# Fetching the first half's turned tiles earlier, and another order of the last batch's four sums

## The chip, the cores and the metric

One Trainium2 chip, one of its cores. The time is device microseconds (us) of one execution of the whole program, inputs and outputs in HBM. The kernel before takes 1034.33 us (median of 3 runs, 1034.21 to 1034.42). The engines are TensorE (PE; its weight loads are PEld), VectorE (DVE), ScalarE (ACT), GpSimd (POOL) and SyncE (SP), which here issues nearly all transfers, in the order of its queue.

## The reference

Sparse attention over 4 batches of 8 heads, 768 positions and 64 channels, followed by a Fourier mixing block. Cut to what is computed:

```python
scores = (q @ k.T) / sqrt(64)                 # per head, 768 x 768
scores = where(mask, scores, -1e9)            # window, first and last blocks, random blocks
attn = softmax(scores) ; x = attn @ v         # heads side by side: x is (4, 768, 512)
mixed = real(fft(fft(x, axis=1), axis=2))
u  = x + mixed
un = (u - mean(u)) / sqrt(var(u) + 1e-6)      # over the 512 channels
out = u + max(un @ w_ch1, 0) @ w_ch2          # w_ch1 is 512 x 2048, w_ch2 2048 x 512
```

## The kernel before

The program runs one batch after another, numbered 0 to 3 here. A batch's attention goes by pairs of heads. While TensorE does the attention of the next batch, the engines carry out the mixing and the two dense layers of the batch before; the last batch's mixing stands alone at the end. A batch's 768 rows are held as two halves, 0 and 1, of three tiles of 128 rows by 512 channels (T is 3).

The order of the work is made when the program is built. A planner keeps three lists. `apart` holds the mixing steps of a batch in a fixed order (`before`, then `after`); `late` holds the dense layers of the batch, eight products `quad` with rounds of `channels` in between (`outputs` in the last batch); `short` holds small steps of the attention. It places their steps between the attention's matmuls by rough costs. Each engine then runs its instructions in exactly the order in which they were written, and waits at the head of its queue.

What the change touches lies between the mixing and the first dense product. The normalised rows `un` must be turned, so that channels lie along the partitions (tile `unT`, one for each half):

- In batches 0 to 2 `un_blocks` (L1021) turns 32 x 32 blocks on VectorE (L1026) and stores the tile to a scratch area in HBM (`far<-un`, L1027). `fetch` (L1031) brings a half back in four pieces of 192 KB (`unT<-far`, L1040). A fetch must wait until the three stores of its half have landed. The six tiles come in the order half 0: 1, 2, 0, then half 1: 1, 2, 0.
- When the first tile of half 1 is stored and at most five items of the batch before are left in `late`, `fetch(0, True)` does not issue the pieces of half 0 but puts them in the list `parts`. They are issued two at a time behind a store of results of a half 0 (`store`, L1306), and whatever is left goes out in `un_back` (L1050), which stands behind the last tile of half 1 and fetches half 1 as well.
- In batch 3 `un_flip` turns the tiles with TensorE and ScalarE copies them (L1009); nothing goes through HBM.

Then `right` (L1071, its instruction is L1085) forms four sums over the turned tiles of both halves, called R1 to R4 here: R1 and R2 give t1 and t2 (the tile `t`), R3 overwrites a part of half 1's `unT`, R4 gives t4 and needs R2's t2. In batches 0 to 2 each of them is one instruction over all three tiles; in batch 3 each is two, a wide one for tiles 1 and 2 and a narrow one for tile 0.

`quad` (L1110) is a product of 2 x 2 blocks in seven matmul groups of four (L1131). Its groups come in this order: `xp` and `yp` from half 0's `unT` alone, `z` from t2, `z` from t1, `z` from R3's result (into the PSUM bank of the first z, and so behind VectorE's addition of it, `hA`, L1136), `yp` from t4, and a last `z`.

Of the kernel before, what the change touches and what calls it, by code (L numbers as in the profile page):

```python
# [104 lines left out]
def kernel(  # L105
# [29 lines left out]
    T = C // 2  # L135
# [858 lines left out]
    def mixer(b, xA, xB):  # L994
# [3 lines left out]
        first, pq, ar, sp, wh = fourier(b, xA, xB, uns)  # L998
        tt = nc.vector.tensor_tensor

        def un_flip(half, m):
            if half not in unT:
                unT[half] = tr_p.tile([P, ND, T * P], FP32, tag="tr", name="unT")
            un = uns.pop((half, m))
            tag, pool = (("t", ps_t), ("m", ps_m))[half == 1 and m != 0]
            tp = pool.tile([P, ND, P], FP32, tag=tag, name="utp")
            for d in range(ND):
                nc.tensor.transpose(tp[:, d, :], un[:, d * P:(d + 1) * P], ident)
            nc.scalar.copy(out=unT[half][:, :, m * P:(m + 1) * P], in_=tp)  # L1009
# [11 lines left out]
        def un_blocks(half, m):  # L1021

            un = uns.pop((half, m))
            if half not in lines:
                lines[half] = far_p.tile([T, P, DM], FP32, tag=f"un{half}", name="far")
            nc.vector.transpose(out=un, in_=un)  # L1026
            by["dma"].dma_start(out=lines[half][m], in_=un)  # L1027
            if half == 1 and len(late) < 2 * T:
                fetch(0, True)

        def fetch(half, by_parts=False):  # L1031

            if half in unT:
                return
            unT[half] = tr_p.tile([P, ND, T * P], FP32, tag="tr", name="unT")
            of = lines[half].rearrange("m (g j) (k a i) -> a j k (m g) i",
                                       j=BLK, a=P // BLK, i=BLK)

            def part(a):
                by["dma"].dma_start(  # L1040
                    out=unT[half][BLK * a:BLK * a + BLK].rearrange(
                        "j k (g i) -> j k g i", i=BLK),
                    in_=of[a])
            for a in range(P // BLK):
                if by_parts:
                    parts.append(lambda a=a: part(a))
                else:
                    part(a)
# [22 lines left out]
        def right(j, *tiles):  # L1071

            spare_room()
            if 1 not in t:
                both = room(4, [P, ND, HS], "t12")
                t[1], t[2], t[3] = both[:, K1, :], both[:, K2, :], unT[1][:, K1, :]
            b11, b21 = unT[0][:, K1, :], unT[0][:, K2, :]
            b12, b22 = unT[1][:, K1, :], unT[1][:, K2, :]

            def part(ap):  # L1080
                return ap.rearrange("p k (t n) -> p k t n", n=P)[:, :, tiles[0]:tiles[-1] + 1, :]

            to, a, c = {1: (t[1], b12, b11), 2: (t[2], b22, t[1]), 3: (b12, b22, b12),
                        4: (t[4], b21, t[2])}[j]
            tt(out=part(to), in0=part(a), in1=part(c), op=ALU.subtract)  # L1085
# [292 lines left out]
        def outputs(r, m, after):  # L1378
# [71 lines left out]
            if r == 1:  # L1450
# [3 lines left out]
        fl = [[("tm"[h == 1 and m != 0], lambda h=h, m=m: un_flip(h, m), 0.6, 0.55, 0.0)  # L1454
               for m in range(T)]
              for h in range(2)]

        ft = [[("d", lambda h=h, m=m: un_blocks(h, m), 0.0, 0.0, 0.7) for m in range(T)]
              for h in range(2)]

# [3 lines left out]
        ri = [[("d", lambda i=i, m=m: right(i, *m), 0.0, 0.0, us) for i in (1, 2, 3, 4)]  # L1464
              for m, us in (((1, 2), RIGHT), ((0,), COMBINE))]
        le = [("d", lambda i=i: left(0, i), 0.0, 0.0, COMBINE) for i in (1, 3, 4)]
        after = ([fl[0][1], sp[1][1]] + le +
                 [fl[0][2], sp[1][2], wh[1][1], fl[0][0], sp[1][0], wh[1][2],
                  fl[1][1], fl[1][2], wh[1][0]] + ri[0] + [fl[1][0]] + ri[1])
        if not last:  # L1470
            before = first + [pq[1], ar[0][1], ar[1][1], sp[0][1],
                              pq[2], wh[0][1], ft[0][1], ar[0][2], ar[1][2], sp[0][2],
# [31 lines left out]
    short, apart, late, due = deque(), deque(), deque(), deque()  # L1504
# [82 lines left out]
    def begin(b):  # L1587


        before, after, rest = mixer(b, x_of[b, 0], x_of[b, 1])  # L1590
        any_of = len(late) + len(apart) + 4 * len(rest)
        hold = 2 * T
        apart.extend((*step, any_of) for step in norm_steps(b) + before)
        apart.extend((*step, hold) for step in after)

        def go():
            late.extend(rest)
        apart.append(("-", go, 0.0, 0.0, 0.0, hold))
# [202 lines left out]
    def general():  # L1801
# [5 lines left out]
        for b in range(B):  # L1807
            xs = [xp.tile([P, T, DM], FP32, tag=tag, name="x") for tag in ("xA", "xB")]
            for h in range(H):
# [43 lines left out]
                for half, x in enumerate(xs):  # L1853
                    sl = slice(half * T, half * T + T)
                    nc.vector.tensor_tensor(out=x[:, :, h * D:(h + 1) * D], in0=op[:, sl, :],
                                            in1=rs[:, sl, :].broadcast_to([P, T, D]),
                                            op=ALU.mult)
            before, after, rest = mixer(b, *xs)
            for step in before + after:
                step[1]()  # L1860
# [44 lines left out]
```

## Time and profile before

| | |
|---|---|
| median of 3 runs | 1034.33 us |
| the profiled execution, its own time | 1034.89 us |
| its span, first to last instruction | 1033.2 us |
| mean granted clock of TensorE | 0.997 |
| TensorE busy | 1011.1 us, 98% |
| VectorE, ScalarE, POOL busy | 713.4, 372.9 and 329.5 us |
| pieces fetched (`unT<-far`) | 24, in the six fetches of batches 0 to 2 |
| share of the 16 transfer engines, SP's and ScalarE's queue together | 26.3% |

In the timelines a row gives start and length in us, engine, line, operation, output and inputs, shape and count; in brackets stands how long the engine sat idle before it and who ended that. Rows of neighbouring instructions of one kind are merged. `SPq` is SP's queue: the row shows how long SP was taken up with issuing, not when the data landed. In rows of stretches (A:B) the busy time and the count of PE, PEld, VectorE, ScalarE and POOL follow the length, then the granted clock of TensorE (1.00 is full speed), the transfer engines' busy share and GB/s.

### The profile page before, as it was taken

The numbers are of one execution on the slowest core, as the hardware profiler recorded it, in microseconds if no ns is written. First come the engines' busy times: TensorE is split into PE (matmuls) and PEld (weight loads), VectorE is DVE, ScalarE is ACT, GpSimd is POOL, SyncE is SP. The second block draws the span as 40 slices with busy tenths as digits, with TensorE's granted clock in tenths as the row PEclk, the third lists the DMA queues.
The fourth block names the chain that finished last, engine by engine and source line by source line (L and its number), as shares of the span: only waits on it lengthen the run. The fifth ranks groups of instructions, "written<-read, shape, count | busy, mean of one in ns | idle before, by whom it ended". The sixth has DMA issues, their size and how long they took to land.

```text
span 1033.2 us, 13060 instructions
## 1 busy us (share of the span) xinstructions
PE 1011.1 (98%) x4526; PEld 561.3 (54%) x4526; DVE 713.4 (69%) x1294; ACT 372.9 (36%) x763; POOL 329.5 (32%) x363
## 2 busy tenths in 40 slices
PE   8999999999999999999999999899999999999997
PEld 4434345444767764443534764444444765578576
DVE  6899895977984767755678578565458565675664
ACT  6998765563222222433440223243220221210210
POOL 1000183657634314544552233256540221000000
PEclk9999999999999999999999999999999999999999
DMA  7867422283000008432320002931010001200001
GB/s 216 227 192 229 107 48 46 52 131 49 1 1 1 11 10 166 89 62 40 67 48 1 1 11 85 144 56 43 16 23 8 1 1 51 41 1 0 1 13 53
DMA packets 182309, 60.46 MB, mean 59 GB/s; under 512 B 163018, under 2 KB 173012, under 8 KB 182236
## 3 DMA queue, kind: packets, MB, share of 16 engines
q1 hardware_dynamic: 181116, 58.95, 26.1%
q8 instruction: 38, 0.62, 0.2%
q10 hardware_dynamic: 1088, 0.59, 0.2%
q14 instruction: 35, 0.29, 0.1%
q0 software_dynamic: 32, 0.01, 0.0%
HBM read 46.14 MB, written 15.73 MB: 60 GB/s over the span
## 4 chain that ended last, share of the span: by engine, by line
PE 79%; DVE 10%; ACT 2%; issue 2%; SPq 2%; DMA 2%; POOL 1%; ACTq 0%; DVEq 0%; POOLq 0%
PE z L1131 16%; PE y L1298 13%; PE s L587 10%; PE o L661 9%; PE yp L1131 7%; PE yy L1392 7%; PE xp L1131 4%; PE yz L1239 3%; PE zp L869 2%; PE yc L1239 2%; SPq L1040 2%; PE yw L1239 2%; PE sp L732 1%; DVE x L939 1%; DVE t L1085 1%
## 5 line engine op out<-in xcount | busy, mean ns | idle before, releaser
L647 POOL TENSOR_TENSOR acc<-acc,e 128x384 f32<-128x384 f32 x160 | 164.1, 1059 | 91.8 <-DVE e L617 72.2
L587 PE MATMUL s<-qT,kT 64*128 64x384 f32 x768 | 153.4, 514 | 5.4 <-ACT e L607 3.7
L661 PE MATMUL o<-e,vr 128*64 128x384 f32 x768 | 142.2, 497 | 0.0
L617 DVE TENSOR_TENSOR e<-s,mask 128x768 f32<-128x768 f32 x86 | 78.2, 950 | 47.7 <-ACT s L615 39.7
L587 PEld LDWEIGHTS s<-qT,kT 64*128 64x128 f32 x768 | 63.8, 185 | 85.9 <-ACT e L607 22.6
L647 POOL TENSOR_TENSOR acc<-e 128x384 f32<-128x384 f32 x42 | 47.7, 1157 | 191.4 <-ACT e L607 121.1
L615 ACT ACTIVATE s<-s 128x768 f32<-128x768 f32 x86 | 65.2, 791 | 107.3 <-PE s L587 107.1
L607 ACT ACTIVATE e<-s 128x768 f32<-128x768 f32 x106 | 80.9, 811 | 52.0 <-PE s L597 34.1
L1131 PE MATMUL z<-unT,t 128*128 128x384 f32 x256 | 93.7, 489 | 2.0 <-DVE hA L1136 2.0
L661 PEld LDWEIGHTS o<-e,vr 128*64 128x64 f32 x768 | 47.7, 136 | 69.8 <-issue 68.5
L1136 DVE TENSOR_TENSOR hA<-z,hA 128x384 f32<-128x384 f32 x64 | 35.6, 556 | 63.9 <-PE z L1131 63.9
L1140 ACT ACTIVATE hA<-hA 128x384 f32<-128x384 f32 x64 | 33.5, 523 | 128.2 <-DVE hA L1136 128.2
L1252 POOL TENSOR_TENSOR x<-of,x 128x256 f32<-128x256 f32 x45 | 39.2, 876 | 124.8 <-ACT of L1244 61.7
L1298 PE MATMUL y<-w_sb,hB 128*128 128x512 f32 x168 | 75.4, 597 | 0.0
L1298 PE MATMUL y<-w_sb,hA 128*128 128x512 f32 x168 | 74.6, 596 | 0.0
L1131 PEld LDWEIGHTS z<-unT,t 128*128 128x128 f32 x256 | 48.6, 191 | 37.8 <-DVE hA L1136 4.7
L1140 ACT ACTIVATE hB<-hB 128x384 f32<-128x384 f32 x64 | 33.5, 523 | 87.3 <-DVE hB L1136 87.3
L1301 DVE TENSOR_TENSOR x<-y,x 128x512 f32<-128x512 f32 x42 | 29.0, 690 | 49.7 <-PE y L1298 49.6
L1298 PEld LDWEIGHTS y<-w_sb,hA 128*128 128x128 f32 x168 | 31.3, 190 | 39.8 <-issue 37.1
L1298 PEld LDWEIGHTS y<-w_sb,hB 128*128 128x128 f32 x168 | 30.9, 190 | 38.6 <-issue 38.6
L1131 PE MATMUL z<-t,w_sb 128*128 128x384 f32 x128 | 46.9, 489 | 3.7 <-DVE t L1085 3.7
L1151 ACT COPY hA<-xp 128x384 f32<-128x384 f32 x32 | 15.3, 478 | 92.6 <-PE xp L1131 90.1
(237 smaller groups left out, 1736.3 us busy)
## 6 DMA issues: line engine op xcount, KB each, us to landing
wraw<-in_moe_w_ch_dram SPq DMA_DIRECT2D x32, 512.0 KB
vr<-in_v_dram SPq DMA_DIRECT2D x30, 192.0 KB
far<-un SPq DMA_DIRECT2D x18, 256.0 KB
unT<-far SPq DMA_DIRECT2D x24, 192.0 KB
qb<-in_q_dram SPq DMA_DIRECT2D x44, 96.0 KB
kb<-in_k_dram SPq DMA_DIRECT2D x44, 96.0 KB
falls<-x SPq DMA_DIRECT2D x9, 256.0 KB
out_dram<-x SPq DMA_DIRECT2D x18, 128.0 KB
```

The costliest lines, as they stand in the source:

```text
L587: nc.tensor.matmul(s[:, i, 0:HS], kT[rows, c * P:(c + 1) * P], qT[rows, queries], start=True, stop=u not in by_pe)
L607: nc.scalar.activation(out=e, in_=s[:, :, 0:HS], func=ACT.Exp, scale=scale)
L615: nc.scalar.activation(out=s[:, :, 0:HS], in_=s[:, :, 0:HS], func=ACT.Exp, scale=scale)
L617: nc.vector.tensor_tensor(out=e, in0=s[:, :, 0:HS], in1=m.broadcast_to([P, 2, HS]), op=ALU.mult)
L647: nc.gpsimd.tensor_add(out=acc[:, i, :], in0=start[:, i, :], in1=e[:, i, :])
L661: nc.tensor.matmul(o[D * i:D * i + D, :], vt[:, i, c, :], e[:, i, :], start=(c == 0), stop=(c == C - 1))
L1131: nc.tensor.matmul(to, a[:, k, :], c[:, k, :], start=(k == 0), stop=(k == ND // 2 - 1))
L1140: nc.scalar.activation(out=h, in_=h, func=ACT.Relu)
L1239: nc.tensor.matmul(to, a[:, k, :], c[:, k, :], start=start and k == 0, stop=k == 1, skip_group_check=True)
L1252: nc.gpsimd.tensor_add(out=to, in0=kept[i], in1=to)
L1298: nc.tensor.matmul(y, hs[0, half][:, l, m * P:(m + 1) * P], w2_sb[:, 4 * r + l, :], start=(l == 0), stop=(l == 3))
L1392: nc.tensor.matmul(ps, a[:, k, :], c[k // 2][:, k % 2, :] if isinstance(c, list) else c[:, k, :], start=(k == 0), stop=(k == 3))
```

## The change

Two edits. In `un_blocks`, the pieces of half 0 are put in `parts` only if more than three items are left in `late`, that is, while a round of half 0 with its stores can still come; with three or fewer, they are issued at once. In the last batch's `after`, R1 and R2 of tiles 1 and 2 stay where they were; the turning of half 1's tile 0 (`fl[1][0]`) and R1 and R2 of tile 0 follow them, and R3 and R4 come behind, first of tiles 1 and 2, then of tile 0.

```diff
@@ un_blocks
             if half == 1 and len(late) < 2 * T:
-                fetch(0, True)
+                fetch(0, len(late) > T)
@@ after, of the last batch
-                  fl[1][1], fl[1][2], wh[1][0]] + ri[0] + [fl[1][0]] + ri[1])
+                  fl[1][1], fl[1][2], wh[1][0]] + ri[0][:2] + [fl[1][0]] + ri[1][:2] +
+                 ri[0][2:] + ri[1][2:])
```

SP's queue in batch 0, at the end of the mixing (`x8` are both halves' pieces together):

```order
 L1027 DMA far<-un 128x512
 L276 DMA vr<-in_v_dram 128x384 x2
-L1027 DMA far<-un 128x512 x2
+L1027 DMA far<-un 128x512
+L1040 DMA unT<-far 32x48x32 x4
+L1027 DMA far<-un 128x512
 L236 DMA qb<-in_q_dram 32x24x32 x4
 L1027 DMA far<-un 128x512
-L1040 DMA unT<-far 32x48x32 x8
+L1040 DMA unT<-far 32x48x32 x4
 L236 DMA kb<-in_k_dram 32x24x32 x4
 L276 DMA vr<-in_v_dram 128x384 x2
```

Half 0's four pieces have moved ahead of half 1's second store, a query load of four pieces and half 1's third store. Half 1's four pieces stay where they were.

SP's queue at the same place of batch 2:

```order
 L1027 DMA far<-un 128x512
 L1317 DMA out_dram<-x 64x512 x2
-L1027 DMA far<-un 128x512 x3
-L1040 DMA unT<-far 32x48x32 x8
+L1027 DMA far<-un 128x512
+L1040 DMA unT<-far 32x48x32 x4
+L1027 DMA far<-un 128x512 x2
+L1040 DMA unT<-far 32x48x32 x4
 L1330 DMA falls<-x 128x512
 L1317 DMA out_dram<-x 1x512
```

Half 0's pieces have moved ahead of two stores of half 1. In batch 1 nothing moves: more than three items are left there, and the pieces still go out two by two.

VectorE in the last batch, ahead of the first product:

```order
 L1085 TENSOR_TENSOR t_5960<-unT 128x2x256
 L1085 TENSOR_TENSOR t_5960<-unT,t_5960 128x2x256
+L1085 TENSOR_TENSOR t_5960<-unT 128x2x128
+L1085 TENSOR_TENSOR t_5960<-unT,t_5960 128x2x128
 L1085 TENSOR_TENSOR unT<-unT 128x2x256
 L1085 TENSOR_TENSOR t_5888<-unT,t_5960 128x2x256
-L1085 TENSOR_TENSOR t_5960<-unT 128x2x128
-L1085 TENSOR_TENSOR t_5960<-unT,t_5960 128x2x128
 L1085 TENSOR_TENSOR unT<-unT 128x2x128
 L1085 TENSOR_TENSOR t_5888<-unT,t_5960 128x2x128
```

The narrow R1 and R2 have moved ahead of the wide R3 and R4. The instructions of TensorE, ScalarE and POOL keep their order.

## The prediction

> **What bounds the kernel now.** I read the page first, then TensorE's waits, the timelines round each long wait, and last the transfers' issue times. The page's busy row:
>
> ```profile
> PE 1011.1 (98%) x4526; PEld 561.3 (54%) x4526; DVE 713.4 (69%) x1294; ACT 372.9 (36%) x763; POOL 329.5 (32%) x363
> ```
>
> TensorE is the bound, and no matmul is added or removed. A gain can only come out of the 22 us in which PE idles (1033.2 - 1011.1), or of matmuls that ran slow. The waits of PE over the whole span name two groups that this change can touch (us in total, times, longest):
>
> ```profile
> PE z L1131 <- DVE t L1085: 3.7, 2, 2.7
> ...
> PE z L1131 <- DVE hA L1136: 2.0, 4, 1.1
> ```
>
> L1085 is `right`, the sums over turned tiles. The 3.7 are 2.69 in batch 2 and 1.03 in batch 3; the 1.1 is in batch 0, behind the same sums. Batch 1's fetch stays in pieces. All transfers here are on SP's queue; POOL's and ScalarE's hold none.
>
> **Batch 2: the fetch.** Timelines of PE and VectorE, then SyncE's queue, POOL, and the granted clock (the 1.00 or 0.57 behind the busy times):
>
> ```profile
> 655.92 1.45 PE L1131 MATMUL yp<-unT,w_sb 128*128 128x384 f32 x4
> ...
> 660.07 1.73 PE L1131 MATMUL z<-t,w_sb 128*128 128x384 f32 x4 [2.69 <-DVE t L1085]
> ...
> 665.71 1.45 PE L1131 MATMUL yp<-t,w_sb 128*128 128x384 f32 x4
> ...
> 654.84 0.69 DVE L1301 TENSOR_TENSOR x<-y,x 128x512 f32<-128x512 f32 x1 [1.79 <-PE y L1298]
> ...
> 657.98 0.96 DVE L1085 TENSOR_TENSOR t<-unT 128x768 f32<-128x768 f32 x1 [2.45 <-DMA falls<-x]
> 658.97 0.96 DVE L1085 TENSOR_TENSOR t<-unT,t 128x768 f32<-128x768 f32 x1
> ...
> 638.19 5.22 SPq L1027 DMA_DIRECT2D far<-un  x3
> ...
> 643.09 0.32 SPq L1027
> ...
> 643.51 10.49 SPq L1040 DMA_DIRECT2D unT<-far  x8
> ...
> 648.11 1.22 SPq L1040
> ...
> 653.39 3.86 POOL L647 TENSOR_TENSOR acc<-acc,e 128x384 f32<-128x384 f32 x4
> ...
> 240.00:260.00 20.00, 18.72 (x63) 10.06 (x62) 17.31 (x26) 4.10 (x9) 11.20 (x8) 1.00 0.03 4
> ...
> 661.00:665.00 4.00, 4.00 (x8) 2.07 (x7) 2.38 (x5) 0.52 (x1) 0.00 (x0) 0.57 0.79 229
> ```
>
> Call the four sums R1 to R4. R1 starts when all eight pieces have landed (its row names `falls<-x`, which is only the transfer that came last), R2 0.99 us later, and z needs R2's result. A group of four matmuls takes 1.29 us when PE does not wait (see z in the last fence), so z could start at 655.92 + 1.29 = 657.21, and starts at 660.07: 2.86 lost. Then the clock falls to 0.57, and z to yp takes 665.71 - 660.07 = 5.64 where three groups make 3.9: by 3 x 1.29 + 0.11 for a first group 1.7 too long. This junction costs 4.5 us.
>
> Now fetch 0 follows the first of the three stores, at 638.19 + 0.32 = 638.5 instead of 643.51. Its four issues took 648.11 - 643.51 = 4.6, so SP is held until 643.1, and the two stores queued behind it go out at 643.1 and 643.4 (the last went at 643.09): 0.3 later. Fetch 1 then waits for the last store to land, behind fetch 0's data. The nearest row for that is batch 1, where the last store goes out behind two fetch pieces:
>
> ```profile
> 398.46 1.26 SPq L1027 DMA_DIRECT2D far<-un  x1
> ...
> 402.69 3.77 SPq L1040 DMA_DIRECT2D unT<-far  x4
> ...
> 410.14 0.96 DVE L1085 TENSOR_TENSOR t<-unT 128x768 f32<-128x768 f32 x1 [1.94 <-DMA unT<-far]
> 411.13 1.64 DVE L1085 TENSOR_TENSOR t<-unT,t 128x768 f32<-128x768 f32 x1
> ...
> 410.24 6.00 POOL L647 TENSOR_TENSOR acc<-acc,e 128x384 f32<-128x384 f32 x4
> ```
>
> Store to fetch 1 is 4.2 us there (402.69 - 398.46), fetch 1 to R1 7.45. So fetch 1 starts at 643.4 + 4.2 = 647.6, half a microsecond before its present 648.11, but with nothing of fetch 0 left ahead of it, and lands at 655.1. Bounds: without a wait it cannot beat the eight pieces' own 657.98 - 643.51 = 14.5, so 653.0; with all four pieces ahead, two more than in batch 1 at 7.45 / 4 each, the store lands 7.9 after its issue and the data at 658.75, 0.8 later than now. I take 655.1, because 643.4 is 4.9 us into the 7.45 of fetch 0, so that less than half of it is left, which is batch 1's backlog. All ends below 655.5 are alike, since the VectorE addition at 654.84 stands ahead of R1 and ends at 655.53.
>
> What is late next is R2 itself. POOL's four additions end at 657.25, and R1 and R2 now run beside them. In batch 1 R1 took 0.99 and R2 1.64 beside such additions, not 0.96. I take these: R2 ends at 655.53 + 0.99 + 1.64 = 658.16, z starts 0.14 behind it (660.07 - 659.93) at 658.3, which gives 1.8 us. A gap of 1.1 is left in place of 2.86. The 1.1 us gap of batch 0 stands beside a clock of 1.00 (the stretch from 240 to 260), so I take the clock loss as gone: 1.7 more. **Batch 2: 3.4 us** (1.77 + 1.66), between -0.8 and 4.1 (R2 at 0.96: z at 657.6).
>
> **Batch 0: the fetch.** SP's queue, ScalarE's use of the query load, VectorE's row, and PE's wait:
>
> ```profile
> 210.97 4.12 SPq L1027 DMA_DIRECT2D far<-un  x2
> ...
> 215.18 2.19 SPq L236 DMA_DIRECT2D qb<-in_q_dram  x4
> ...
> 219.72 0.34 SPq L1027 DMA_DIRECT2D far<-un  x1
> ...
> 224.65 0.84 ACT L544 ACTIVATE qT<-qb 128x768 f32<-128x768 f32 x1
> ...
> 235.31 1.73 DVE L1085 TENSOR_TENSOR t<-unT 128x768 f32<-128x768 f32 x1 [4.55 <-issue]
> ...
> 241.98 1.74 DVE L642 TENSOR_TENSOR acc<-acc,e 128x768 f32<-128x768 f32 x1
> 243.64 1.50 DVE L554 STREAM_TRANSPOSE kT<-kb 128x768 f32<-128x768 f32 x1
> 245.01 0.52 DVE L1136 TENSOR_TENSOR hA<-z,hA 128x384 f32<-128x384 f32 x1
> ...
> 243.07 1.45 PE L1131 MATMUL z<-t,t 128*128 128x384 f32 x4
> 245.59 1.56 PE L1131 MATMUL z<-unT,t 128*128 128x384 f32 x4 [1.06 <-DVE hA L1136]
> ```
>
> VectorE runs without a break from R1 at 235.31 to hA at 245.01, and PE waits for that hA: z could start at 243.07 + 1.29 = 244.36, so 1.23 us are to be had if R1 comes 1.23 earlier. Fetch 0 now goes out from 211.3 to 215.9 (4.6 as above). The second-half store and the query load behind it slip by 0.7; their data slip by fetch 0's backlog, at most 7.45 - 4.6 = 2.9 after its issue. The query pieces, issued by 218.1, are first read at 224.65, so they stay covered. That cover ends if they take over 6 us; then ScalarE and PE pay one for one. The last store, at 219.72, waits for VectorE and does not move; with 4.2 and 7.45 R1 can start at 231.4, 3.9 earlier, three times what is needed. The key load behind the fetch goes out earlier as well. **Batch 0: 1.2 us**, between 0 (POOL's additions, slowed by the earlier sums, hold back the acc at 241.98) and 1.5 (the next, 0.2 us wait goes too).
>
> **Batch 3: the sums' order.** No fetch here; ScalarE writes the turned tiles.
>
> ```profile
> 881.87 1.45 PE L1131 MATMUL yp<-unT,w_sb 128*128 128x384 f32 x4
> 884.35 1.56 PE L1131 MATMUL z<-t,w_sb 128*128 128x384 f32 x4 [1.03 <-DVE t L1085]
> 885.75 1.45 PE L1131 MATMUL z<-t,t 128*128 128x384 f32 x4
> 887.03 1.45 PE L1131 MATMUL z<-unT,t 128*128 128x384 f32 x4
> ...
> 880.26 1.10 ACT L1009 COPY unT<-utp 128x512 f32<-128x512 f32 x2 [0.42 <-PE utp L1008]
> ...
> 882.22 0.68 DVE L1085 TENSOR_TENSOR unT<-unT 128x512 f32<-128x512 f32 x1
> ...
> 883.42 0.42 DVE L1085 TENSOR_TENSOR t<-unT 128x256 f32<-128x256 f32 x1
> 883.87 0.42 DVE L1085 TENSOR_TENSOR t<-unT,t 128x256 f32<-128x256 f32 x1
> ...
> 884.55 0.42 DVE L1085 TENSOR_TENSOR t<-unT,t 128x256 f32<-128x256 f32 x1
> ```
>
> z needs R2 of all three tiles, the row at 883.87, which ends at 884.29. Now the narrow R1 takes the slot at 882.22 (its last tile has been copied at 881.36), the narrow R2 starts 0.45 later, as at 883.42 and 883.87, and ends at 883.09; with 0.06 (884.35 - 884.29) z starts at 883.16, the end of yp's 1.29: 1.19 earlier. The wide R3 and R4 move behind it. They are late next, but all eight still end at 884.97. R3's reader z (887.03 now) would want it at 885.74; hA (z's addition) fits in between, starting at 885.0 and ending at 885.6. **Batch 3: 1.2 us**, bounds 1.03 (PE's idle alone) and 1.19.
>
> **Sum.** 3.4 + 1.2 + 1.2 = 5.8 us. PE's order is the same throughout, so what is won at a junction is kept until a later wait takes it, and those left on PE after it are below 1 us each. The profiled execution took 1034.89, 0.56 above the median: 1029.1 by it, 1034.33 - 5.8 = 1028.5 by the median.
>
> **Rivals.** B: the sums collide with POOL and the clock still falls. R1 takes 1.73 as the R1 of batch 0 does, R2 1.64; z starts at 659.1. For it: POOL is busy just then; against: batch 1's R1 took 0.96. That leaves a gap of 1.9, between the 1.06 of batch 0 without a loss and 2.69 with one. Gain 1.0 + 2.4, time 1030.9; had the clock held, 1029.3. The Trainium skill (SBUF — State Buffer, "SBUF: two separate sides") says that a VectorE operation with two SBUF inputs and a GpSimd one lock a shared port pair for a whole instruction, and the other waits; batch 1's 1.64 agrees. The Trainium skill (TensorE: Matmul & The Clock Gate, "What's actually happening") puts the fall of the clock behind an idle window of about 3.4 us; by that B would give 1029.3, but the trace differs: it shows a fall after 2.69.
>
> A: the transfers' gain is eaten by the store's wait. With 7.9 us from last store to fetch 1, R1 in batch 2 is 0.8 late and in batch 0 0.2 early (219.72 + 7.9 + 7.45 = 235.07); with batch 3's 1.2 the net is 0.6, time 1033.7. For it: four pieces stand ahead, not two; against: they get 4.6 us to drain before the store.
>
> C: the same wait decides the other way. With X us from the last store's issue to fetch 1, R1 is X - 7.1 late in batch 2 and X - 8.1 in batch 0, against 1.2 won: even at X = 8.2, slower by 0.2% from X = 9.3. At 10 it gives 1037.9. It needs over twice the 4.2 seen.
>
> D: the fetch is moved but covered, and the sums change nothing: 1034.3. Against it, both waits stand in PE's own rows.
>
> **Chances.** 0.2%, about what a measurement of this kernel can tell, is 2.1 us: 1032.3 and 1036.4. Forecast 0.60 (its own range 1027.5 to 1029.6); B 0.20; A 0.12, of which 0.05 stays below 1032.3; C 0.05; D 0.03. Faster 0.60 + 0.20 + 0.05 = 0.85, same 0.07 + 0.03 = 0.10, slower 0.05. The range runs from 1026.8, a little below the upper bounds' 6.8 together, to 1032.4.
>
> **What would show it.** Batch 2: SP issues four fetches at about 638.5, R1 near 655.5 (shifted by batch 0's gain), PE's gap about 1 and no clock below 1.00 behind it. Batch 0: R1 near 231.4 and no 1.06 wait. Batch 3: no wait of z on L1085. Wrong if SP sits for over 7 us before fetch 1, or if the clock still falls.

## The result, and the profile after

The changed kernel takes 1030.72 us (median of 7 runs, 1029.99 to 1031.07) against 1034.21 us (7 runs, 1033.50 to 1034.75) for the kernel before on the same chip: a ratio of 0.9967, 95% interval 0.9956 to 0.9977, or 3.5 us less. In a later session it was 1030.06 (5 runs) against 1034.56 (9 runs), ratio 0.9958 (0.9944 to 0.9972). Faster, as forecast, but 2.2 us short of the 1028.5 that was predicted. Two runs that took far longer than all others are left out of every time and count here: one of the kernel before at 1481.57 us, one of the kernel with R1 twice at 2089.70. The profiled execution of after took 1030.72 itself, with a span of 1029.0 us.

The waits of PE over the whole span, kernel after (us in total, times, longest):

```profile
PE z L1131 <- DVE t L1085: 1.6, 1, 1.6
...
PE z L1131 <- DVE hA L1136: 1.1, 3, 0.5
```

The two waits on L1085 (3.7 us together) have become one of 1.6, and the 1.1 us wait for hA in batch 0 is gone. PE itself is busy for 1010.2 us (1011.1 before).

Spans can't be subtracted as they stand, because the two executions do not open alike. The timeline of PE round the first scores, first the kernel before, then after:

```profile
6.37 1.73 PE L323 MATMUL warm<-ident 128*128 128x128 f32 x14
8.02 1.56 PE L587 MATMUL s<-qT,kT 64*128 64x384 f32 x8
```

```profile
6.80 2.41 PE L323 MATMUL warm<-ident 128*128 128x128 f32 x14
9.13 1.56 PE L587 MATMUL s<-qT,kT 64*128 64x384 f32 x8
```

The same 14 warming matmuls took 0.7 us longer, and the first scores start 1.11 us later, though no instruction of that stretch was touched. Counted from these scores on, the span went from 1033.2 - 8.02 = 1025.2 to 1029.0 - 9.13 = 1019.9: 5.3 us. So in this pair of executions 5.3 us were won, and in the medians 3.5. Both numbers need an explanation; the three places that the change touches (the junctions, one in each of batches 2, 0 and 3) come first.

**Batch 2.** Kernel after: SP's queue, VectorE, POOL, PE and the granted clock.

```profile
638.86 4.32 SPq L1040 DMA_DIRECT2D unT<-far  x4
643.22 1.78 SPq L1027 DMA_DIRECT2D far<-un  x2
648.38 3.98 SPq L1040 DMA_DIRECT2D unT<-far  x4
...
654.86 0.69 DVE L1301 TENSOR_TENSOR x<-y,x 128x512 f32<-128x512 f32 x1 [1.79 <-PE y L1298]
656.19 0.96 DVE L1085 TENSOR_TENSOR t<-unT 128x768 f32<-128x768 f32 x1 [0.64 <-DMA falls<-x]
657.18 1.63 DVE L1085 TENSOR_TENSOR t<-unT,t 128x768 f32<-128x768 f32 x1
...
653.41 4.58 POOL L647 TENSOR_TENSOR acc<-acc,e 128x384 f32<-128x384 f32 x4
...
654.65 1.45 PE L1131 MATMUL xp<-unT,w_sb 128*128 128x384 f32 x4
...
658.96 1.53 PE L1131 MATMUL z<-t,w_sb 128*128 128x384 f32 x4 [1.56 <-DVE t L1085]
...
662.90 1.45 PE L1131 MATMUL yp<-t,w_sb 128*128 128x384 f32 x4
...
660.00:665.00 5.00, 5.00 (x17) 3.01 (x16) 4.41 (x9) 1.05 (x2) 0.00 (x0) 1.00 0.74 184
```

Half 0's pieces go out where they were forecast, at 638.86. The gap in front of z is 1.56 instead of 2.69, and the clock behind it stays at 1.00. In the kernel before `xp` starts at 654.63, so `xp` to the second `yp` was 665.71 - 654.63 = 11.08 and is 662.90 - 654.65 = 8.25 now: 2.83 us, of which 1.13 is the shorter gap and 1.70 the clock. In the kernel before, taken in finer stretches, the clock stands at half for 3.50 us and nowhere else in the junction, and half of that is 1.75:

```profile
661.20:664.70 3.50, 3.50 (x7) 1.80 (x6) 1.88 (x4) 0.52 (x1) 0.00 (x0) 0.51 0.75 228
```

This is called a fall from here on. It begins 1.1 us after z has started, when PE is busy again.

**Batch 0.** Kernel after: SP's queue, VectorE's R1, POOL, and PE.

```profile
212.50 5.26 SPq L1040 DMA_DIRECT2D unT<-far  x4
...
221.72 0.46 SPq L1027 DMA_DIRECT2D far<-un  x1
225.22 3.88 SPq L1040 DMA_DIRECT2D unT<-far  x4
...
234.01 1.28 DVE L1085 TENSOR_TENSOR t<-unT 128x768 f32<-128x768 f32 x1 [2.13 <-DMA unT<-far]
...
231.55 7.94 POOL L647 TENSOR_TENSOR acc<-acc,e 128x384 f32<-128x384 f32 x6 [3.53 <-DVE acc L642]
...
244.19 1.45 PE L1131 MATMUL z<-t,t 128*128 128x384 f32 x4
245.48 1.45 PE L1131 MATMUL z<-unT,t 128*128 128x384 f32 x4
```

The first z with a wait of 1.06 before now follows its forerunner at once. From the first scores on it starts at 245.48 - 9.13 = 236.35, against 245.59 - 8.02 = 237.57 before: 1.2 us, which is what was forecast.

**Batch 3.** Kernel after, VectorE and PE:

```profile
879.85 0.42 DVE L1085 TENSOR_TENSOR t<-unT,t 128x256 f32<-128x256 f32 x1
880.20 0.68 DVE L1085 TENSOR_TENSOR unT<-unT 128x512 f32<-128x512 f32 x1
...
879.06 1.45 PE L1131 MATMUL yp<-unT,w_sb 128*128 128x384 f32 x4
880.35 1.54 PE L1131 MATMUL z<-t,w_sb 128*128 128x384 f32 x4
881.73 1.45 PE L1131 MATMUL z<-t,t 128*128 128x384 f32 x4
```

The narrow R2 ends at 880.27 and z starts at 880.35, 1.29 behind `yp`, where before it started 2.48 behind (884.35 - 881.87): 1.19 us. Nothing that moved behind it is waited for.

1.2 + 2.83 + 1.19 = 5.2, which accounts for the 5.3 between the profiled executions. What it does not account for is the 3.5 between the medians.

### The profile page after: what moved, and what is told of

Read it like the earlier page. It is cut to its first block, busy times and chain, and to the rows that moved or that the text cites. A ratio compares the mean times of both kernels' runs of the same rounds, so it can differ in the third digit from the quotient of the medians.

```text
span 1029.0 us, 13054 instructions
## 1 busy us (share of the span) xinstructions
PE 1010.2 (98%) x4526; PEld 561.6 (55%) x4526; DVE 713.8 (69%) x1294; ACT 372.9 (36%) x763; POOL 330.3 (32%) x363
## 4 chain that ended last, share of the span: by engine, by line
PE 83%; DVE 9%; ACT 2%; issue 2%; DMA 2%; POOL 1%; SPq 1%; ACTq 0%; DVEq 0%; POOLq 0%
PE z L1131 16%; PE y L1298 13%; PE s L587 11%; PE o L661 10%; PE yp L1131 8%; PE yy L1392 7%; PE xp L1131 4%; PE yz L1239 3%; PE zp L869 2%; PE yc L1239 2%; PE yw L1239 2%; PE sp L732 1%; PE s L597 1%; DVE x L939 1%; ACT e L607 1%
```

## The experiments

Each kernel was timed beside the kernel before, in the same session and on the same chip. There were three more sessions: one for the two edits apart, one, on another chip than the others, for the clock and the first run of two and two pieces, and one for the last four kernels. The names of the theories in the expectations hold for the runs of one session; the edits are shown against the kernel named.

### The two edits apart

The first edit alone, on the kernel before:

```diff
-                fetch(0, True)
+                fetch(0, len(late) > T)
```

> The fetch edit alone, in batches 0 and 2; the order of the last batch's sums is as before. Theory 1 (the three junctions add up, the slow clock behind batch 2's gap comes only in some executions, and the 1.1 us by which the profile of after opens later is chance): the median is lower by 1.2 (batch 0) + 1.2 (batch 2, the gap alone) = 2.4 us, at most 4.1 if most executions of before have the slow clock. Theory 2 (every changed program opens 1.1 us later, and the slow clock is always there): 1.2 + 2.9 - 1.1 = 3.0 us lower, and its profile shows the first attention scores at about 9.1 us, not 8.0.

Measured: 1031.42 us (8 runs, 1031.13 to 1032.04), ratio 0.9975 (0.9964 to 0.9985), 2.8 us below before, between theory 1's 2.4 and theory 2's 3.0. Its profile has the first scores at 8.61 us, neither at 8.0 nor at 9.1.

The second edit alone (the order of batch 3's sums):

> The new order of the last batch's sums alone; the fetches are as before. Theory 1: lower by 1.2 us. Theory 2: lower by 1.2 - 1.1 = 0.1 us. In both, z of batch 3 has no wait on L1085 (1.03 before).

Measured: 1033.08 us (11 runs, 1032.13 to 1033.56), ratio 0.9987 (0.9978 to 0.9996), 1.1 us, theory 1's 1.2 and not theory 2's 0.1; z of batch 3 has no wait on L1085 any more. The parts add up: 2.8 + 1.1 = 3.9, beside 3.5 and 4.5 for both in two sessions.

The kernel with the second edit alone leaves batch 2 as it was, and this profile was the first surprise. PE and the granted clock:

```profile
661.17 1.53 PE L1131 MATMUL z<-t,w_sb 128*128 128x384 f32 x4 [2.62 <-DVE t L1085]
...
660.00:665.00 5.00, 3.83 (x12) 2.39 (x13) 4.73 (x8) 0.52 (x1) 0.00 (x0) 1.00 0.87 184
```

The gap of 2.62 is there, the slow clock is not. So the 1.7 us behind the gap are not paid by every execution.

The fetch edit in batch 0 alone:

```diff
-                fetch(0, True)
+                fetch(0, b > 0 or len(late) > T)
```

> The fetch edit in batch 0 alone; batch 2's pieces and the last batch's sums are as before. Theory 1: lower by 1.2 us, and batch 2's junction is that of before (gap 2.7, the clock behind it slow or not). Theory 2: lower by 1.2 - 1.1 = 0.1 us. If batch 0's gain is lost again before batch 1, as VectorE's and POOL's queues allow, both give 0.

Measured: 1032.51 us (11 runs, 1031.70 to 1034.87), ratio 0.9987 (0.9978 to 0.9996). The runs fall into two groups, eight from 1031.70 to 1032.67 and three from 1034.56 to 1034.87. The profiled one took 1034.58:

```profile
659.76 1.77 PE L1131 MATMUL z<-t,w_sb 128*128 128x384 f32 x4 [2.84 <-DVE t L1085]
...
660.00:665.00 5.00, 5.00 (x11) 2.71 (x11) 3.33 (x6) 0.52 (x1) 0.00 (x0) 0.66 0.67 150
```

An execution of the upper group shows the slow clock. The groups' means are 2.4 us apart (1032.3 and 1034.7), somewhat more than the 1.7 of a fall; that the other two runs of the upper group fell as well is inferred from their times. The median, 1.7 below before, is 0.5 more than batch 0's 1.2, but the mean is 1.3 below (1032.95 against 1034.23), which fits.

The kernel before once more:

> The kernel before, unchanged, once more with a profile of its own. Both theories: ratio 1.000 within 0.1%. Theory 1: the opening (scores first at 8.0 or at about 9.1 us) and the clock behind batch 2's gap (0.57 in 661 to 665 or 1.00) need not be those of the first profile. Theory 2: both are the same as in the first profile.

Measured: 1034.64 us (11 runs, 1032.93 to 1036.06), ratio 1.0003 (0.9994 to 1.0012). The profiled execution, 1035.28, had the slow clock again:

```profile
660.43 1.59 PE L1131 MATMUL z<-t,w_sb 128*128 128x384 f32 x4 [2.68 <-DVE t L1085]
...
660.00:665.00 5.00, 4.57 (x9) 2.55 (x10) 3.52 (x6) 0.52 (x1) 0.00 (x0) 0.68 0.75 162
```

Its first scores are at 8.27 us, where the first profile had 8.02. So theory 2, by which the opening belongs to the program and the fall to every execution, is out: the kernel with the second edit alone had no fall, and no changed kernel profiled after this opens at 9.1 us.

### Does the clock fall in every execution?

In the kernel before, PE is given something to do in the gap: ten products of the identity with itself (two matmuls each in the trace) into the bank that the next z overwrites.

```diff
+            for _ in range(10 if b == 2 and p == 0 else 0):
+                nc.tensor.matmul(z7[:, 0:P], ident, ident, start=True, stop=True)
```

> The kernel before, with ten matmuls of the identity into the first z's own PSUM bank in batch 2, between yp and z (about 2.3 us of the 2.86 that PE loses there; z overwrites them). No data moves. Theory 1 (the gap of 2.7 us leaves a slow clock behind it in about a third of the executions, 1.8 us each): the clock behind the junction is 1.00 in the profile, the slow executions are gone, so that the highest run stays below 1034.8 (1035.36 for before), and the median falls by 0.3 to 0.8 us. Rival (every execution of before pays the slow clock): the median falls by 1.7 to 1.8. Rival (the slow clock has another cause than the gap): no change, and 0.57 again in the profile or slow executions as before.

Measured: 1034.13 us (11 runs, 1032.88 to 1035.15), against 1034.40 for before, ratio 0.9998 (0.9989 to 1.0007). Profiled, PE and clock:

```profile
658.18 2.39 PE L1157 MATMUL z<-ident 128*128 128x128 f32 x20
660.95 1.56 PE L1131 MATMUL z<-t,w_sb 128*128 128x384 f32 x4 [0.38 <-DVE t L1085]
...
660.00:665.00 5.00, 4.62 (x19) 2.84 (x18) 4.63 (x7) 0.52 (x1) 0.00 (x0) 1.00 0.94 200
```

In the profiled execution the clock held, as it should. The times hardly show it: the median is 0.27 lower, a little under what was expected, and the highest run is above the bound that was set. By the interval the kernel is at most 1.1 us faster, so the rival by which every execution pays 1.7 is out.

The mean granted clock of each run, which is on record beside its time, does show it. It has a second source, seen behind the last matmul (it ends at 1023.31 in the profile of after, at 1026.55 in that of the kernel with PE kept busy), where PE sits idle until the program ends. After:

```profile
1023.31:1025.31 2.00, 0.00 (x0) 0.00 (x0) 0.42 (x1) 0.00 (x0) 0.00 (x0) 1.00 0.52 136
1025.31:1029.00 3.69, 0.00 (x0) 0.00 (x0) 0.00 (x0) 0.00 (x0) 0.00 (x0) 0.51 0.15 42
```

PE kept busy:

```profile
1026.55:1031.45 4.90, 0.00 (x0) 0.00 (x0) 0.42 (x1) 0.00 (x0) 0.00 (x0) 1.00 0.33 87
1031.45:1032.40 0.95, 0.00 (x0) 0.00 (x0) 0.00 (x0) 0.00 (x0) 0.00 (x0) 0.51 0.00 0
```

The clock falls here in all 14 profiles, from 2.0 to 4.9 us after the last matmul has ended, and no matmul is left to pay for it. It takes 0.0005 to 0.0018 off the mean of an execution; a fall behind batch 2's gap takes 0.0017 more (1.75 of 1033 us). So by this estimate a run at 0.999 or above had no fall in the gap, one at 0.997 or below had one, and 0.998 can be either. The profiles agree: the four with a fall are at 0.995 to 0.997, the ten without at 0.998 to 1.000.

With PE kept busy all eleven runs are at 0.999 or 1.000. Of the 28 runs of before beside them eleven are, eleven are at 0.998 and six at 0.997. Every run with PE kept busy or with a profiled gap of at most 1.83 us, 52 in all, is at 0.998 or above. So the gap is what makes the clock fall. Of the 78 runs of before with a clock on record, 20 are at 0.997 and 28 at 0.998: by the same estimate a fall came in at least a quarter of the executions and in at most six of ten, and the kernel before pays it by chance. In time the runs at 0.997 stand 1.1 to 1.8 us above those at 0.999 or more, by the means of each set.

Then the changed kernel with a longer gap, by making batch 2's R1 twice and four times with the same result (2 here, 4 in the second kernel):

```diff
-            tt(out=part(to), in0=part(a), in1=part(c), op=ALU.subtract)
+            for _ in range(2 if b == 2 and j == 1 else 1):
+                tt(out=part(to), in0=part(a), in1=part(c), op=ALU.subtract)
```

> The kernel after, with R1 of batch 2 run twice (0.9 to 1.0 us more ahead of R2): the gap of PE grows from 1.56 to about 2.5 us. Theory 1: the executions fall apart into two groups again, about 1.8 us apart, the larger one near 1031.7 and the smaller near 1033.5; median about 1.0 to 1.5 us above that of after. Rival (the gap's length does not matter for the clock): one group, 1.0 us above after.

> The kernel after, with R1 of batch 2 run four times: the gap grows to about 4.2 us. Theory 1 with a clock that needs idle time in its own window of about 3.5 us: every execution now has the slow clock, the median is 2.6 + 1.8 = 4.4 us above after (about 1035.1) with one group. Rival (chance of one in three whatever the gap): median 2.6 above after (about 1033.3) with a smaller group 1.8 above.

Measured with R1 twice: median 1031.46 us (10 runs), ratio 0.9981 (0.9971 to 0.9990). Six runs lie between 1031.12 and 1031.50 and four between 1033.02 and 1034.81, again 2.4 us apart by their means; the six have clocks of 0.998 and 0.999, the four 0.996 and 0.997. With R1 four times: 1035.59 us (11 runs, 1034.92 to 1036.03), ratio 1.0011 (1.0002 to 1.0020), one group, all at 0.995 to 0.997, 4.9 above the changed kernel's 1030.72 in the result above. Both are as theory 1 has it: the rivals had one group for the first kernel and 1033.3 for the second. The first kernel's PE and clock, then the second's:

```profile
659.34 1.53 PE L1132 MATMUL z<-t,w_sb 128*128 128x384 f32 x4 [2.82 <-DVE t L1086]
...
660.00:665.00 5.00, 5.00 (x17) 2.95 (x16) 4.41 (x10) 0.79 (x2) 0.00 (x0) 1.00 0.76 178
```

```profile
661.71 2.90 PE L1132 MATMUL z<-t,w_sb 128*128 128x384 f32 x4 [4.58 <-DVE t L1086]
...
660.00:665.00 5.00, 3.29 (x5) 1.85 (x6) 3.55 (x5) 0.00 (x0) 0.00 (x0) 0.50 0.89 209
```

With R1 twice the gap is 2.82, longer than before's 2.69, and in this execution the clock held. With R1 four times it is 4.58; 4.58 - 1.56 = 3.0 of the 4.9 is the gap, and the 1.9 left is about the price of a fall, which by the clocks every run paid. So a gap of 2.6 to 2.9 us makes the clock fall in some executions and not in others, and one of 4.6 in all eleven. In the Trainium skill (TensorE: Matmul & The Clock Gate, "What's actually happening") the clock falls after an idle window of about 3.4 us. The falls here came behind gaps of 2.68, 2.69 and 2.84, which are shorter than that, and behind the last matmul after 2.0 to 4.9 us; the measurement decides here.

### What is left of the gap in batch 2

First, two of half 0's pieces at once and two behind half 1's last store, so that the store has less ahead of it (against the changed kernel):

```diff
-                fetch(0, len(late) > T)
+                fetch(0, True, 0 if len(late) > T else 2)
...
-        def fetch(half, by_parts=False):
+        def fetch(half, by_parts=False, now=0):
...
-                if by_parts:
+                if by_parts and a >= now:
```

> The kernel after, with only two of half 0's four pieces issued at once in batches 0 and 2, the other two behind half 1's last store. If the last store lands late because four pieces stand ahead of it (5.2 us from its issue to fetch 1 in the profile of after), it now lands while the other two pieces are issued, fetch 1 follows without a wait, and R1 of batch 2 starts near 655.5 instead of 656.2: gap 0.6 to 0.7 shorter, median 0.6 below after (1030.1), batch 0 as in after. Rival (the bytes, not the wait, set the landing): R1 no earlier than in after, median the same or up to 0.5 above.

Measured: 1030.15 us (5 runs, 1029.82 to 1030.88), ratio 0.9960 (0.9947 to 0.9973). VectorE, POOL and PE:

```profile
654.15 0.69 DVE L1301 TENSOR_TENSOR x<-y,x 128x512 f32<-128x512 f32 x1 [1.79 <-PE y L1298]
654.76 1.67 DVE L1085 TENSOR_TENSOR t<-unT 128x768 f32<-128x768 f32 x1
656.46 1.63 DVE L1085 TENSOR_TENSOR t<-unT,t 128x768 f32<-128x768 f32 x1
...
652.72 4.57 POOL L647 TENSOR_TENSOR acc<-acc,e 128x384 f32<-128x384 f32 x4
...
658.24 1.53 PE L1131 MATMUL z<-t,w_sb 128*128 128x384 f32 x4 [1.54 <-DVE t L1085]
```

The data now come in time: R1 starts right behind the addition, without the 0.64 of idle time. But the gap is 1.54, about the changed kernel's 1.56, because R1 now takes 1.67 and not 0.96, beside POOL's additions. Whether these additions are the cause was tested by leaving six of them out, with either way of fetching, beside both kernels with them. The two kernels without them do not compute the whole result: three of the six tiles of one accumulator are missing from its sum.

```diff
-        start = e_of[u - 1] if c == 1 else acc
+        few = (n, half) == (13, 0); start = e_of[u - 1] if c == (4 if few else 1) else acc
...
-            for i in range(2):
+            for i in range(0 if few and c < 4 else 2):
                 nc.gpsimd.tensor_add(out=acc[:, i, :], in0=start[:, i, :], in1=e[:, i, :])
```

> The changed kernel itself, beside the next three. Theory 1 (in batch 2 half of what the junction still loses is the late landing of fetch 1, the other half R2 running beside POOL's additions): 1030.7 us as before, PE's gap in front of the first z of batch 2 1.5 to 1.6, R1 starting 1.5 us after xp's start, R1 about 0.99 and R2 about 1.63. Rival (the gap is set by something that varies from execution to execution): another gap, by more than 0.3.

> Two pieces of half 0 at once, two behind the last store, as in the run of that kind before, now beside the changed kernel on the same chip. Theory 1: the earlier data is eaten by R1 and R2 both beside POOL's additions, so the time is within 0.5 us of the changed kernel's and the gap 1.4 to 1.7. Rival (the earlier median of 1030.15 was a gain of its own): 0.5 us or more below the changed kernel again.

> The changed kernel, but the six additions of POOL that run while batch 2's sums R1 and R2 are made (650 to 658 us) are left out; three of the six tiles of one accumulator are so missing from its sum. All transfers stay. Theory 1: R1 still starts 1.5 us after xp's start because it waits for the data, R2 takes 0.97 instead of 1.63, the gap is 0.9 instead of 1.56, time 0.7 below the changed kernel. Rival (POOL's additions have nothing to do with R2's length): R2 stays at 1.6 and the gap at 1.5.

> Both: two and two pieces, and the six additions of POOL left out. Theory 1: R1 starts 0.8 after xp's start, R1 and R2 take 0.97 each, z waits 0.2 to 0.4 at most, xp to the second yp of the quad 7.0 instead of 8.25, time 1.2 us below the changed kernel. Rival (something else holds R1 or z): a gap of 0.9 or more is left.

Measured, with `xp` to the second `yp` of the junction from each profile's PE timeline:

| fetch of half 0, POOL's six additions | gap before z | xp to yp | span from the first scores on | median (runs) |
|---|---|---|---|---|
| four at once, kept (changed kernel again) | 1.82 | 8.51 | 1020.3 | 1030.06 (5) |
| two and two, kept | 1.54 | 8.23 | 1020.1 | 1031.03 (6) |
| four at once, left out | 1.04 | 7.73 | 1019.2 | 1030.29 (5) |
| two and two, left out | 0.15 | 6.84 | 1018.6 | 1029.53 (5) |

The ratios to before are, in the order of the rows, 0.9958 (0.9944 to 0.9972), 0.9968 (0.9955 to 0.9980), 0.9960 (0.9945 to 0.9974) and 0.9950 (0.9936 to 0.9964). VectorE in the first row's kernel, in the third's, and in the fourth's, with PE's wait there:

```profile
656.39 1.53 DVE L1085 TENSOR_TENSOR t<-unT 128x768 f32<-128x768 f32 x1 [1.00 <-DMA falls<-x]
657.95 0.96 DVE L1085 TENSOR_TENSOR t<-unT,t 128x768 f32<-128x768 f32 x1
```

```profile
655.61 0.96 DVE L1085 TENSOR_TENSOR t<-unT 128x768 f32<-128x768 f32 x1 [0.80 <-DMA falls<-x]
656.61 0.96 DVE L1085 TENSOR_TENSOR t<-unT,t 128x768 f32<-128x768 f32 x1
```

```profile
655.01 0.95 DVE L1085 TENSOR_TENSOR t<-unT 128x768 f32<-128x768 f32 x1
656.00 0.96 DVE L1085 TENSOR_TENSOR t<-unT,t 128x768 f32<-128x768 f32 x1
...
657.10 1.53 PE L1131 MATMUL z<-t,w_sb 128*128 128x384 f32 x4 [0.15 <-DVE t L1085]
```

The first row missed what was expected of it: R1 started 1.90 us after `xp` and took 1.53, R2 0.96, where R1 was to start after 1.5 and R2 to be the slow one. The same kernel's gap was 1.56 in its first profile, so one profile tells a gap to no better than 0.3.

Without POOL's additions both sums take 0.95 or 0.96. One cause removed leaves a gap of 1.54 or 1.04, both removed leave 0.15: the gap is made of the late data and of the slowed sums, and the two hide each other, since earlier data only bring more of the sums beside POOL. The Trainium skill (SBUF — State Buffer, "SBUF: two separate sides") describes a port pair that a VectorE operation with two SBUF inputs and a GpSimd one lock for a whole instruction; 0.96 against 1.53 to 1.67 agrees with that. So does the first profile of after, where R1 kept its 0.96 beside POOL and POOL's four additions took 4.58 instead of the 3.86 of before: there, by the same lock, POOL would have waited for R1, and R2 (1.63) for POOL.

In the times less of it is seen. The third row was expected 0.7 below the first and lies 0.2 above in the median, where the spans from the first scores on have it 1.1 below; the fourth is 0.5 below, not 1.2. Five or six runs each, that spread over 1.1 to 1.7 us, don't tell such differences. The 1030.15 of the first run with two and two, on the other chip, did not come again (1031.03), so that kernel isn't shown to be better than the changed one, and no kernel that computes the whole result is.

## Why the prediction was right, and where not

**Batch 3, right.** 1.19 us forecast, 1.19 in the rows, 1.1 alone by the medians.

**Batch 0, right in size, with the slack misjudged.** 1.2 us forecast and found. R1 was to start at 231.4, which with the later opening is 232.5, and started at 234.01. The last store was not to move, but went out at 221.72, which is 0.9 later than 219.72 with the opening taken off: the query load ahead of it on SP's queue held it up, since that load began 2.65 later (218.94 against 215.18, less 1.11) and not 0.7. The store to fetch 1 took 3.5 us (221.72 to 225.22), less than the 4.2 used, but fetch 1 to R1 took 8.8 and not 7.45. This cost nothing, because R1 was forecast 3.9 us earlier where 1.23 were needed, and 2.4 were left. POOL's six additions beside the sums took 7.94 (5.79 in the same place before), the condition under which the gain was to vanish; VectorE's `acc` still followed R4 without a wait.

**Batch 2, the gap: forecast 1.77, measured 1.13.** The step that failed is "fetch 1 starts at 647.6 and lands at 655.1". It started at 648.38, and R1 at 656.19. SP was taken up with the two stores from 643.22 to 645.00, where the forecast had the second go out at 643.4, and the wait behind them was 3.4 from the end of that row, 5.2 from its start; the rows don't part the stores' issue from their landing. Together that is 0.8 late, and R1 came 7.8 behind the issue instead of 7.45. R1 was thus 0.66 later than the 655.53 of the forecast. The opening and batch 0's gain cancel here (+1.11 and -1.2), so the times can be compared as they stand. R2's 1.63 beside POOL was forecast as 1.64. Rival A's mechanism, a fetch 1 held up by the store, was therefore there, but 0.8 us of it and not the 3.7 (7.9 against 4.2) that it needed. Rival B, both sums slowed, a gap near 1.9 and a fall behind it, did not come in the first profile; in the later one R1 did take 1.53, with R2 at 0.96 and a gap of 1.82, and there too the clock held. That the median lies 0.2 from B's 1030.9, nearer than from the forecast, is chance: the fall that B counts on is in no profile of the changed kernel.

**Batch 2, the clock: forecast 1.66, worth less to the median.** The mechanism and its price were right: 1.70 between the two profiled executions, and none of the profiles of after shows a fall. What failed is the step from there to "1034.33 - 5.8 = 1028.5 by the median". It takes the whole loss out of a median that holds it only in part: the gap of 2.69 stood just where the clock falls in some executions and holds in others. By the clocks on record a fall came in between a quarter and six in ten of the executions of before, in four of ten with R1 twice, and never with PE kept busy; and keeping PE busy in the gap, which by the clocks removes all falls, took 0.27 off the median, by its interval at most 1.1, and not 1.66. Leaving the fall out, 1.2 + 1.13 + 1.19 = 3.5, the difference of the medians in the result above.

How much of the fall the times hold stays open. The mean of before is 1034.3 over the 74 runs beside the other kernels of all sessions, that of after 1030.5 over its 12 runs: 3.8 us, which leaves 0.3 for the falls, where a quarter to six in ten of 1.7 us would be 0.4 to 1.0. The openings hint at why: of the five profiles with before's fetch in batch 2, the three with a fall have their first scores at 8.02 to 8.27 us, the two without at 8.69 and 8.77, so that executions with a fall may open earlier. Five profiles don't show that.

A hint stood in the numbers: the profiled execution was 0.56 above the median and above every run shown then. The prediction took it as a shift of everything ("1029.1 by it") and did not scale the clock's term down for it.

Of the rivals, C (slower by the store's wait) and D (nothing) did not happen. The range to 1032.4 held the time; the forecast's own range from 1027.5 to 1029.6 did not.

## What to carry to other kernels

A loss that a profile shows behind a gap (here 1.7 us of slow clock) belongs to that execution; before it is taken off a median, ask whether the gap lies where the loss comes by chance, and whether the profiled execution stands above the median. A run's mean clock, where it is recorded, can tell this without another profile. Two causes in a row can hide each other: earlier data took 0.3 us off the gap here, VectorE's sums free of POOL 0.8, both together 1.7, because each alone only runs into the other (counted from the 1.82 of the second profile of after; from the 1.56 of the first it is 0.0, 0.5 and 1.4). And a store that is queued behind a fetch had its own issue slowed as well as its landing (1.78 us for two, where one with no fetch ahead took 0.32), so price both for whoever waits for it.

## What was unexpected of the hardware

- The opening of the program varies: the first scores start between 8.02 and 9.13 us over the profiled executions of all these kernels, with the same instructions ahead of them. 1.1 us is a third of what the change brought, and a span has to be counted from behind it.
- The clock does not fall at one length of a gap. Gaps of 1.83 us and less, and of 2.62 and 2.82, left it at 1.00; gaps of 2.68, 2.69, 2.84 and 4.58 were followed by 0.50 to 0.68 over the five microseconds from 660 to 665. Behind the last matmul it held for 2.0 to 4.9 us of idle time.
- It falls when PE is already busy again: 1.1 to 1.3 us after z had started in the three profiles with a gap of 2.7 to 2.8, and then for 3.5 us at half speed, 1.7 us of time. The groups of run times lie 2.4 apart, and the 0.7 more was not traced.
- The kernel before spreads over 3.5 us (1032.92 to 1036.44, 74 runs), the changed one over 1.3 (1029.76 to 1031.08, 12 runs). Falls are not all of that: with PE kept busy and no fall, eleven runs still spread over 2.3 us. What else varies was not traced.
